# The last inverse unit of a fused SSM convolution: two writes and two of its four reads issued from ScalarE's queue

## The chip, the core and the metric

The kernel runs on one core of one Trainium2 chip, as a single launch in float32. The metric is the device time of that launch in microseconds. One execution is also recorded by the profiler, and the places below are given in microseconds from the start of that recording.

## The reference

Two S4 layers (A and B) convolve the same input `u` (2048 positions, 512 channels) with kernels built from 128 complex states each, and a gate mixes the two results:

```python
dt = jnp.exp(log_dt)[:, None]
P = jnp.exp((dt * (A_re + 1j * A_im))[:, :, None] * l[None, None, :])
K = jnp.einsum("dn,dnl,dn->dl", Cc, P, dt * Bc).real
Kf, Uf = rfft(K, 2 * L), rfft(u, 2 * L)          # zero-padded to twice the length
y = irfft(Uf * Kf, 2 * L)[..., :L] + u * Dskip
...
g = sigmoid((x * gate_w).sum(-1, keepdims=True))
return g * a + (1 - g) * b
```

## The kernel before

The 512 channels are worked in eight chunks (`c` from 0 to 7) of 64 channels, both layers together. For each chunk `tables` builds the time kernels (POOL, ScalarE and VectorE make sines and exponentials, TensorE multiplies them), `first` and `spectrum` transform them in two stages, `conv` multiplies with the spectrum of `u`, and `back` and `fin` transform back. All of that is interleaved over the chunks.

The end of the last chunk (`c` = 7) is what the change touches. `back(7, U)` for the units `U` = 0 to 3 does the first half of the inverse transform: 64 matmuls (`L721`) into a pair of PSUM banks, two copies (`L300` on ScalarE or `L302` on VectorE) into the tile `z`, two DMA writes of 256 KB each from `z` into the scratch `zb` in device memory, and then reads of `zb` back into SBUF in another layout, into the tile that is called `xa` here. Units 0 to 2 are read whole, 512 KB each. Unit 3, the last, is read in four quarters of 128 KB, one for each of the four final matmul groups. `fin(7, k)` is such a group: 32 matmuls (`L757`, `c<-xa,gsi`) that need the quarter `k` of unit 3 and the whole of units 0 to 2, then one copy, then one DMA of 128 KB to the output. The groups run as `k` = 3, 2, 1, 0. The outputs of chunk 6 (`fin(6, k)`, matmuls `c<-f,gsi`) are finished in the same stretch. Between them `stay_awake` runs twelve matmuls (`L770`) whose result nobody reads.

Nothing is scheduled by rule here. Every operation is recorded with a number by `Plan.__call__`, and the table of numbers `ORDER` gives the one order in which all are laid down; each engine takes its own in that order. An operation with two engines to choose from runs on the second if its number carries a `b`. In the tail, 1879 and 1880 are the two writes of unit 3; 1869 is the whole read of unit 2; 1884, 1883, 1882 and 1881 are the quarters 3, 2, 1 and 0 of unit 3; 1968, 1959 and 1965 are the output DMAs of chunk 6 for `k` = 3, 0 and 2, and 1962 the one for `k` = 1.

All DMAs are issued by SyncE (SP in the profile), but for those that `dma` is told may go to ScalarE (ACT):

```python
op("sp act" if also_act else "sp", "dma", size,
   lambda e: (sp if e == "sp" else act).dma_start(out=out(), in_=in_()), reads, writes, touch=touch)
```

A queue issues in order: an instruction that waits holds everything behind it on its engine. Eight semaphores (`DMAHW0` to `DMAHW7` in the instructions' waits) are dealt to the DMAs of both queues in rotation, and a DMA is issued only when the DMA that had its semaphore before it has landed. So a DMA can wait for one whose data it doesn't use.

Of the kernel before, what the change touches and what calls it, by code (L numbers as in the profile page):

```python
# [150 lines left out]
1811 1380 1394 1406 1382 1812 1407 1408 1820 1819 1837 1785 1798 1846 1802 1803 1800 1813 1801 1814 1947 1395b 1396 1873 1956  # L151
1849 1818 1786 1788 1409b 1410 1381b 1411 1821 1825 1413 1826b 1828 1412 1827 1829 1817 1816 1815 1787 1835 1836 1838 1847
1850 1839 1840 1862 1859 1841 1848 1851 1852 1842 1853 1854 1863 1860 1831 1832 1843 1844 1833 1830 1874 1871 1864 1957 1855
1856 1845 1865 1875 1872 1866 1876 1867 1868 1857 1877 1878b 1960 1966 1967b 1981 1963 1968b 1958b 1964b 1879 1880 1869 1884
1978 1883 1959 1975 1882 1965b 1972 1881 1961 1962 1969 1979 1980 1976 1973 1977 1970 1974 1971
"""


# [49 lines left out]
def ssm_mix(ctx: ExitStack, tc: tile.TileContext, a, out, dry=False):  # L208
# [58 lines left out]
    def t(*key):  # L267
        if key not in tiles:
            shape, dtype = shapes[key[0]]
            tiles[key] = pools[key[0]][slot[key]].tile(shape, dtype, name=key[0])  # L270
        return tiles[key]
# [21 lines left out]
    def dma(size, out, in_, reads, writes, also_act=False, touch=()):  # L293
        op("sp act" if also_act else "sp", "dma", size,
           lambda e: (sp if e == "sp" else act).dma_start(out=out(), in_=in_()), reads, writes, touch=touch)

    def copy(n, o, i, reads, writes, touch=()):
        def emit(e):
            if e == "act":
                act.activation(out=o(), in_=i(), func=AF.Copy)  # L300
            else:
                dve.tensor_copy(out=o(), in_=i())  # L302

        op("act dve", "copy", n, emit, reads, writes, touch=touch)
# [402 lines left out]
    def back(c, U):  # L707

        last = c == NCH - 1
        ys = [("y", c, 2 * U + i) for i in range(2)]  # L710
        ps = [(("s", "sq")[U % 2], "inv", U)] if last else [("c", "inv", c, U, x) for x in range(2)]
        bank_of = lambda x: t(*ps[0]).rearrange("p a b -> p (a b)")[:, 512 * x:512 * x + 512] if last else t(*ps[x])

        def inv(_):
            for q in range(4):
                for h in range(2):
                    for x in range(2):
                        for e in range(2):
                            f = 2 * q + e
                            v = t("vv", U // 2)[64 * x:64 * x + 64, 8 * (U % 2) + f]  # L720
                            pe.matmul(bank_of(x)[64 * e:64 * e + 64, CH * q:CH * q + CH], v[:, 0:64] if h else v[:, 32:96],  # L721
                                      t(*ys[f // 4])[64 * x:64 * x + 64, h, :, f % 4], start=h == 0, stop=h == 1,
                                      tile_position=(64 * x, 64 * e))

        op("pe", "inv", 128, inv, [*ys, ("vv", U // 2)], ps, table="square")
        z, zb, f = ("z", c, U), ("zb", c), home(c)
        for x in range(2):
            copy(512, lambda x=x: t(*z)[:, x].rearrange("p q k -> p (q k)"), lambda x=x: bank_of(x), [ps[0 if last else x]],
                 [z] * (x == 0) + [("zx", c, U, x)], [z] * x)
        new = U == 0  # L730
        for x in range(2):
            g = 8 * U + 4 * x
            dma(256, lambda g=g: t(*zb)[g:g + 4].rearrange("g p k -> p g k"), lambda x=x: t(*z)[:, x],
                [("zx", c, U, x)], [zb] * (new and x == 0) + [("zu", c, U, x)], touch=[z] + [zb] * (not (new and x == 0)))
        whole = last and U < 3
        for h in range(1 if whole else 4):
            a0, an = (0, 32) if whole else (8 * h, 8)
            dma(512 if whole else 128, lambda a0=a0, an=an: t(*f)[32 * U:32 * U + 32, a0:a0 + an],
                lambda a0=a0, an=an: t(*zb)[8 * U:8 * U + 8].rearrange("g (m a) k -> (g m) a k", m=4)[:, a0:a0 + an],
                [("zu", c, U, 0), ("zu", c, U, 1)],  # L740
                [f] * (new and h == 0) + [("fu", c, U, i) for i in (range(4) if whole else (h,))],
                touch=[zb] + [f] * (not (new and h == 0)))

    def home(c):
        return ("f", c) if c < NCH - 1 else ("xa", "fin")
# [49 lines left out]
    for T in range(NT):  # L795
        c, g = divmod(T, NG)
# [8 lines left out]
    for c in range(NCH):  # L805
        for j in range(NJ):
            conv(c, j)
            if j % 2:
                back(c, j // 2)
# [48 lines left out]
```

## Time and profile before

| | us |
|---|---|
| median of 3 runs | 434.33 (433.04 to 438.38) |
| the profiled execution's own time | 429.2 |
| its span, first to last instruction | 427.4 |
| busy in the span: PE / DVE / ACT / POOL | 384.0 / 385.1 / 361.3 / 358.7 |
| granted TensorE clock, mean | 0.994 |

The profiled execution was quicker than the three runs. Its span leaves out 1.8 us around the first and last instruction. Until about 396 us all four engines are nearly always busy. In the last 15.4 us (412.0 to 427.4) PE is busy 9.81 us, DVE 0.66 and ACT 1.92, and what is left is writes, reads and outputs.

In the rows below, `SPq` and `ACTq` are DMA issues from SyncE and ScalarE, with the time of issue and how long the issuing took. A row of DMA issues has a count, the KB of each, and the time from issue to landing.

### The profile page before, as it was taken

What the parts mean: (1) busy time and instruction counts of PE and PEld (TensorE: products, weight loads), DVE (VectorE), ACT (ScalarE), POOL (GpSimd) and SP (SyncE); (2) the same over time, 40 slices, a digit from 0 to 9 for tenths busy, and PEclk for the clock granted to TensorE, in tenths of its full rate; (3) what the DMA queues carried; (4) which work ended last, traced back from release to release, by engine and by line L of the source; (5) the groups of instructions that cost most, each with busy time, mean ns of one, the idle gap of its engine ahead of it and who ended that gap; (6) DMA issues with size and microseconds to landing.
All of it is one profiled execution on the core that took longest, in us unless ns stands there. A gap on an engine that the chain in (4) does not pass through costs nothing.

```text
span 427.4 us, 21919 instructions
## 1 busy us (share of the span) xinstructions
PE 384.0 (90%) x9636; PEld 342.3 (80%) x9636; DVE 385.1 (90%) x547; ACT 361.3 (85%) x522; POOL 358.7 (84%) x291
## 2 busy tenths in 40 slices
PE   5898887899998989998989999999889979999994
PEld 5787776788877878888979988888778969898964
DVE  5799999999999999998989999999999999996620
ACT  2889999899998999998889989999899898992211
POOL 1896989899999999997999999999999999970000
PEclk9999999899999999999999999999999999999999
DMA  7968845178882677687385555574777576667794
GB/s 240 287 214 269 263 149 180 28 221 224 257 247 79 197 215 203 201 240 230 109 221 177 176 170 156 166 220 145 225 209 217 143 220 199 172 205 216 219 274 137
DMA packets 79855, 84.63 MB, mean 198 GB/s; under 512 B 7600, under 2 KB 62768, under 8 KB 79664
## 3 DMA queue, kind: packets, MB, share of 16 engines
q1 hardware_dynamic: 79472, 82.96, 65.9%
q8 instruction: 76, 1.25, 1.3%
q10 hardware_dynamic: 288, 0.26, 0.2%
q14 instruction: 19, 0.16, 0.1%
HBM read 51.55 MB, written 31.65 MB: 195 GB/s over the span
## 4 chain that ended last, share of the span: by engine, by line
PE 32%; ACT 23%; DVE 15%; POOL 11%; issue 10%; DMA 7%; SPq 1%; ACTq 0%; DVEq 0%; POOLq 0%
PE c L625 8%; PE c L612 8%; PE c L721 6%; PE c L595 5%; POOL ang L277 4%; DVE mr L287 4%; ACT s L290 4%; POOL mr L277 4%; ACT sq L290 4%; ACT ang L290 3%; PE c L757 3%; DVE ei L277 3%; ACT z L300 2%; DMA zb<-z 2%; DVE y L701 2%
## 5 line engine op out<-in xcount | busy, mean ns | idle before, releaser
L287 DVE SCALAR_TENSOR_TENSOR mr<-sq,mr 128x1024 f32<-128x1024 f32 (+1 forms) x128 | 117.5, 946 | 3.1 <-ACT sq L290 3.0
L277 POOL TENSOR_TENSOR mr<-ml 128x1024 f32<-128x1024 f32 x52 | 101.6, 1955 | 2.5 <-PE c L595 2.0
L277 DVE TENSOR_TENSOR ei<-s,mr 128x1024 f32<-128x1024 f32 x64 | 77.6, 1213 | 2.6 <-POOL mr L277 1.0
L595 PE MATMUL c<-mr 128*32 128x64 f32 x2048 | 64.5, 223 | 8.0 <-DVE mr L287 3.0
L290 ACT ACTIVATE s<-ang 128x1024 f32<-128x1024 int32 x64 | 66.2, 1035 | 6.0 <-DVE ei L287 3.4
L277 POOL TENSOR_TENSOR ang<-sa 128x512 int32<-128x512 int32 x64 | 69.8, 1092 | 0.3
L277 POOL TENSOR_TENSOR ang<-par,cint 128x512 int32<-128x512 int32 x64 | 67.2, 1052 | 3.1 <-ACT sq L290 3.1
L701 DVE TENSOR_TENSOR y<-c,u 128x1024 f32<-128x1024 f32 x57 | 68.7, 1214 | 1.1 <-PE c L625 0.8
L290 ACT ACTIVATE ang<-ang 128x1024 f32<-128x1024 int32 x64 | 67.9, 1061 | 0.9
L290 ACT ACTIVATE sq<-ang 128x1024 f32<-128x1024 f32 x64 | 66.1, 1033 | 2.9 <-DVE mr L287 1.5
L277 POOL TENSOR_TENSOR mr<-mh 128x512 f32<-128x512 f32 x64 | 68.3, 1071 | 0.0
L595 PE MATMUL c<-ei 128*32 128x64 f32 x2048 | 63.6, 221 | 1.4 <-issue 1.4
L612 PE MATMUL c<-small,kt 128*64 128x128 f32 x1024 | 63.0, 275 | 1.6 <-ACT z L300 0.9
L595 PEld LDWEIGHTS c<-mr 128*32 128x32 f32 x2048 | 48.4, 110 | 19.0 <-issue 10.0
L721 PE MATMUL c<-y,vv 64*64 64x128 f32 x1792 | 57.9, 273 | 3.9 <-issue 2.6
L612 PEld LDWEIGHTS c<-small,kt 128*64 128x64 f32 x1024 | 55.5, 137 | 5.4 <-ACT z L300 1.3
L625 PE MATMUL c<-xa,w 128*128 128x128 f32 x384 | 53.0, 284 | 4.6 <-ACT z L300 2.3
L721 PEld LDWEIGHTS c<-y,vv 64*64 64x64 f32 x1792 | 50.1, 133 | 8.4 <-issue 3.7
L625 PE MATMUL c<-xb,w 128*128 128x128 f32 x384 | 51.9, 283 | 5.3 <-DVE c L420 1.6
L625 PEld LDWEIGHTS c<-xb,w 128*128 128x128 f32 x384 | 45.7, 191 | 10.7 <-issue 2.4
L625 PEld LDWEIGHTS c<-xa,w 128*128 128x128 f32 x384 | 45.9, 191 | 9.4 <-ACT z L300 2.9
L595 PEld LDWEIGHTS c<-ei 128*32 128x32 f32 x2048 | 50.4, 111 | 1.6 <-issue 1.5
(108 smaller groups left out, 594.5 us busy)
## 6 DMA issues: line engine op xcount, KB each, us to landing
zb<-z SPq DMA_DIRECT2D x64, 256.0 KB, 3.6
u<-us SPq DMA_DIRECT2D x57, 256.0 KB, 4.1
f<-zb SPq DMA_DIRECT2D x112, 128.0 KB, 3.9
us<-z SPq DMA_DIRECT2D x32, 256.0 KB, 3.1
uin<-in_uk_dram SPq DMA_DIRECT2D x16, 256.0 KB, 4.1
f<-in_ut_dram SPq DMA_DIRECT2D x8, 512.0 KB, 5.6
out_dram<-o SPq DMA_DIRECT2D x28, 128.0 KB, 3.2
par<-prd SPq DMA_DIRECT2D x7, 320.0 KB, 4.2
```

Source lines behind the costliest of these rows:

```text
L277: lambda e: (dve if e == "dve" else pool).tensor_tensor(out=out(), in0=in0(), in1=in1(), op=o),
L287: lambda _: dve.scalar_tensor_tensor(out=out(), in0=in0(), scalar=s, in1=in1(), op0=o0, op1=o1), reads, writes, port=port)
L290: op("act", "act", n, lambda _: act.activation(out=out(), in_=in_(), func=func, **{k: v() if callable(v) else v for k, v in kw.items()}), ...
L300: act.activation(out=o(), in_=i(), func=AF.Copy)
L595: pe.matmul(ps[32 * j:32 * j + 32, o], x[:, 4 * o + j, 64:96], x[:, 4 * o + j, 0:64], start=part == 0, stop=part == 1, tile_position=(0, 3 ...
L612: pe.matmul(t(*ps[g // 4])[64 * r:64 * r + 64, 128 * (g % 4):128 * (g % 4) + 128], t(*x)[:, g], t("small")[:, 128 * r:128 * r + 128], star ...
L625: pe.matmul(view()[:, :, k], t("w2", j // 2)[:, 4 * (j % 2) + k], t(*x1)[:, 4 * j + k], start=True, stop=True)
L701: op("dve", "tt1", 1024, lambda _: dve.tensor_tensor(out=t(*y).rearrange("p h s f d -> p h s (f d)"), in0=fv().rearrange("p s f d -> p s ( ...
L721: pe.matmul(bank_of(x)[64 * e:64 * e + 64, CH * q:CH * q + CH], v[:, 0:64] if h else v[:, 32:96], t(*ys[f // 4])[64 * x:64 * x + 64, h, :, ...
L757: pe.matmul(t(*ps)[64 * r:64 * r + 64, DC * i:DC * i + DC], t("gsi")[:, 4 * k + i, s, 64 * r:64 * r + 64], t(*f)[:, 8 * k + 2 * i + r, DC ...
```

## The change

The two writes of unit 3 may now be issued by ScalarE, and they are: they stand behind the one of the two `z` copies of that unit that ScalarE makes. Of the four quarter reads 1883 and 1881 (`k` = 2 and 0) go to ScalarE's queue too, 1884 and 1882 stay on SyncE's. The outputs of chunk 6 keep their engines but stand elsewhere: 1968 behind the writes on ScalarE, 1959 behind the quarter reads on SyncE, 1965 behind the quarter reads on ScalarE. The data, the sizes and the matmuls are the same.

```diff
-1856 1845 1865 1875 1872 1866 1876 1867 1868 1857 1877 1878b 1960 1966 1967b 1981 1963 1968b 1958b 1964b 1879 1880 1869 1884
-1978 1883 1959 1975 1882 1965b 1972 1881 1961 1962 1969 1979 1980 1976 1973 1977 1970 1974 1971
+1856 1845 1865 1875 1872 1866 1876 1867 1868 1857 1877 1878b 1960 1966 1967b 1981 1963 1958b 1879b 1880b 1968b 1964b 1869 1884
+1978 1883b 1975 1882 1972 1881b 1959 1965b 1961 1962 1969 1979 1980 1976 1973 1977 1970 1974 1971
...
             dma(256, lambda g=g: t(*zb)[g:g + 4].rearrange("g p k -> p g k"), lambda x=x: t(*z)[:, x],
-                [("zx", c, U, x)], [zb] * (new and x == 0) + [("zu", c, U, x)], touch=[z] + [zb] * (not (new and x == 0)))
+                [("zx", c, U, x)], [zb] * (new and x == 0) + [("zu", c, U, x)],
+                last and U > 2, touch=[z] + [zb] * (not (new and x == 0)))
...
-                [f] * (new and h == 0) + [("fu", c, U, i) for i in (range(4) if whole else (h,))],
+                [f] * (new and h == 0) + [("fu", c, U, i) for i in (range(4) if whole else (h,))], last and U == 3,
                 touch=[zb] + [f] * (not (new and h == 0)))
```

On SyncE's queue near the program's end there stood, before, from the writes of unit 2 (out of `z_7576`) over the whole read of unit 1 and the writes of unit 3 (out of `z_7619`) to the whole read of unit 2 and the four quarter reads:

```order
L295 DMA zb_7507<-z_7576 128x4x128 [waits DMAHW1_49,Activation_49]
L295 DMA zb_7507<-z_7576 128x4x128 [waits Activation_49]
L295 DMA xa_7574<-zb_7507 32x4096 [waits DMAHW7_49,DMAHW6_49]
L295 DMA zb_7507<-z_7619 128x4x128 [waits DMAHW5_49,Activation_49]
L295 DMA zb_7507<-z_7619 128x4x128 [waits DVE_49]
L295 DMA xa_7574<-zb_7507 32x4096 [waits DMAHW2_49,DMAHW1_49,DMAHW0_49]
L295 DMA xa_7574<-zb_7507 32x1024 [waits DMAHW7_49,DMAHW5_49]
L295 DMA xa_7574<-zb_7507 32x1024
L295 DMA out_0_dram<-o_7683 128x256 [waits DMAHW3_49,DVE_49]
L295 DMA xa_7574<-zb_7507 32x1024 [waits DMAHW4_49]
L295 DMA xa_7574<-zb_7507 32x1024
```

The whole read of unit 2, the second `32x4096` row, waited for the two writes of unit 2 (`DMAHW1` and `DMAHW2`) and for the DMA that had its own semaphore before it, `DMAHW0`, which is the whole read of unit 0. At the same place there stands now:

```order
L295 DMA zb_7507<-z_7576 128x4x128 [waits Activation_49]
L295 DMA zb_7507<-z_7576 128x4x128 [waits DMAHW4_49,Activation_49]
L295 DMA xa_7574<-zb_7507 32x4096 [waits DMAHW7_49,DMAHW6_49,DMAHW5_49]
L295 DMA xa_7574<-zb_7507 32x4096 [waits DMAHW4_49,DMAHW2_49,DMAHW1_49]
L295 DMA xa_7574<-zb_7507 32x1024 [waits DMAHW3_49]
L295 DMA xa_7574<-zb_7507 32x1024
L295 DMA out_0_dram<-o_7682 128x256 [waits DMAHW5_49,DVE_49]
```

The writes of unit 3 and two quarters are gone from this queue. The writes of unit 2 now carry `DMAHW2` and `DMAHW4`, and the whole read of unit 2 waits for these and for `DMAHW1`. On ScalarE's queue at the end, from the copy of unit 3 into `z_7619` on, the difference is:

```order
 L300 ACTIVATE z_7619<-sq_7583 128x512 [waits DMAHW6_49,DMAHW7_49,PE_49,Activation_49]
-L295 DMA out_0_dram<-o_7656 128x256 [waits DMAHW4_49,DVE_49]
-L295 DMA out_0_dram<-o_7685 128x256 [waits DVE_49]
-L300 ACTIVATE o_7747<-c_7622 128x256 [waits DMAHW5_49,DMAHW3_49,PE_49]
+L295 DMA zb_7507<-z_7619 128x4x128 [waits DMAHW1_49,Activation_49]
+L295 DMA zb_7507<-z_7619 128x4x128 [waits DVE_49]
+L295 DMA out_0_dram<-o_7656 128x256 [waits DVE_49]
+L295 DMA xa_7574<-zb_7507 32x1024 [waits DMAHW3_49,DMAHW1_49]
+L295 DMA xa_7574<-zb_7507 32x1024 [waits DMAHW0_49]
+L295 DMA out_0_dram<-o_7687 128x256 [waits DMAHW2_49,DVE_49]
+L300 ACTIVATE o_7747<-c_7622 128x256 [waits DMAHW5_49,PE_49]
```

Here `DMAHW1` and `DMAHW3` are the two writes of unit 3, since the quarter read behind them waits for both. The first write holds `DMAHW1`, the semaphore for which the whole read of unit 2 on the other queue waits too: in the rotation that read comes eight DMAs behind it, and the count it asks for is the one that this write brings.

## The prediction

> **What bounds the kernel now.** I read the stretches first, to see where in the span this change lies.
>
> ```profile
> core 0: us, PE busy (x) PEld busy (x) DVE busy (x) ACT busy (x) POOL busy (x), PEclk, DMA share, GB/s
> 0.00:380.00 380.00, 342.84 (x8704) 306.99 (x8707) 363.52 (x520) 347.91 (x498) 356.89 (x290) 1.00 0.67 197
> ...
> 412.00:427.40 15.40, 9.81 (x172) 6.65 (x170) 0.66 (x2) 1.92 (x5) 0.00 (x0) 0.96 0.60 175
> ```
>
> For 380 us the engines themselves are the limit, and nothing there is touched. What the change can move lies in the last 15.4 us, where VectorE and ScalarE have hardly any work. Then I read the chain of waits of that end.
>
> ```profile
> 407.51 1.95 PE sq L721 x64
> ...
> 409.53 0.60 ACT z L300
> 410.14 0.02 issue
> 410.16 0.70 DVE z L302
> 410.86 0.02 issue
> 410.88 5.03 DMA zb<-z
> ...
> 416.85 2.74 DMA out_dram<-o
> ...
> 419.65 3.96 PE c L757 x128
> ```
>
> Last inverse matmuls, two copies, second write of unit 3 (5.03 us), reads of it, last four matmul groups: from 409.5 to 419.65 the kernel waits for transfers. The step through the output at 416.85 I don't believe, since no matmul needs an output. What the matmuls at 419.65 need are the whole reads and quarter 3. So I asked for the issues one by one, from SyncE's queue and ScalarE's:
>
> ```profile
> 410.15 0.36 SPq L295 DMA_DIRECT2D zb<-z  x1
> 410.88 0.39 SPq L295 DMA_DIRECT2D zb<-z  x1
> 411.94 0.38 ACTq L295 DMA_DIRECT2D out_dram<-o  x1
> 412.97 0.32 SPq L295 DMA_DIRECT2D xa<-zb  x1
> 415.97 0.32 SPq L295 DMA_DIRECT2D xa<-zb  x1
> 416.34 0.41 SPq L295 DMA_DIRECT2D xa<-zb  x1
> 416.85 0.37 SPq L295 DMA_DIRECT2D out_dram<-o  x1
> 417.27 0.42 SPq L295 DMA_DIRECT2D xa<-zb  x1
> 417.74 0.41 SPq L295 DMA_DIRECT2D xa<-zb  x1
> 418.36 0.34 ACTq L295 DMA_DIRECT2D out_dram<-o  x1
> ```
>
> These are write 1 and write 2 of unit 3, an output, the whole read of unit 2, quarters 3 and 2, an output, quarters 1 and 0, an output. The DMA issues of a narrow window give the time to landing of the first five of them, in the same order:
>
> ```profile
> zb<-z SPq DMA_DIRECT2D x1, 256.0 KB, 5.1
> zb<-z SPq DMA_DIRECT2D x1, 256.0 KB, 5.0
> out_dram<-o ACTq DMA_DIRECT2D x1, 128.0 KB, 4.4
> xa<-zb SPq DMA_DIRECT2D x1, 512.0 KB, 5.8
> xa<-zb SPq DMA_DIRECT2D x1, 128.0 KB, 3.4
> ```
>
> So write 1 lands at 410.15 + 5.1 = 415.25, write 2 at 415.9, the output at 416.3, the whole read of unit 2 at 412.97 + 5.8 = 418.8, quarter 3 at 415.97 + 3.4 = 419.4, and the matmuls start 0.25 later. Each lands behind the one issued before it: quarter 3 comes 0.6 behind the whole read of unit 2. The end of the kernel hangs on that whole read nearly as much as on the writes.
>
> **The change part by part.**
>
> *The two writes on ScalarE.* The copy on ScalarE ends at 409.53 + 0.60 = 410.13 and write 1 is issued at 410.15; VectorE's ends at 410.86 and write 2 is issued at 410.88. There are 0.02 us to win at each, and issuing costs 0.38 on ScalarE against 0.36 and 0.39 here. Write 2 waits for VectorE's copy on either queue. I take 0.
>
> *Their landing.* If the two queues share one line of work, 415.25 and 415.9 stay. Whether ScalarE's queue gets past SyncE's is told by its output at 411.94: it took 4.4 us where the same size later takes
>
> ```profile
> out_dram<-o SPq DMA_DIRECT2D x1, 128.0 KB, 1.8
> out_dram<-o ACTq DMA_DIRECT2D x1, 128.0 KB, 2.9
> ```
>
> (issued at 421.28 and at 418.36). With 2.9 it would have landed at 414.8; it landed at 416.3, 0.4 behind write 2, which SyncE had issued 1.06 before it. So ScalarE's queue did not overtake, and I take 0.
>
> [...]
>
> *The new wait.* The whole read of unit 2 stays on SyncE. Before it was issued at 412.97, just when the second write of unit 2 had landed; now it asks for write 1's semaphore as well and can't be issued before 415.25: 2.28 us later. Behind it on SyncE stand quarters 3 and 1, which wait for write 2 until 415.9 anyway, and all later outputs. The cost is less than 2.28, because of its 5.8 us much was queueing behind the writes (2.9 us, until 415.9). The other two whole reads, issued at 405.25 and 408.17, and the write in front of the first, issued at 403.76, give the scale:
>
> ```profile
> xa<-zb SPq DMA_DIRECT2D x1, 512.0 KB, 5.3
> xa<-zb SPq DMA_DIRECT2D x1, 512.0 KB, 6.4
> zb<-z SPq DMA_DIRECT2D x1, 256.0 KB, 3.3
> ```
>
> The first took 5.3 with 1.8 us of queue in front (that write landed at 407.06). After the change there is 1.05 in front (the output until 416.3). If queueing counts one to one, the read takes 5.3 - 1.8 + 1.05 = 4.55 and lands at 419.8, against 418.8: +1.0. Lower bound: nothing in front counts, 3.5 us, 418.75, no loss. Upper bound: 5.8 as now, 421.05, +2.25. I take +1.0, from the read with the queue most like it.
>
> *The reads of unit 3.* Two queues issue the quarters two at a time, quarters 3 and 2 at about 415.95 and quarters 1 and 0 at about 416.35, where the last went at 417.74 before. Nothing waited for these in the old trace:
>
> ```profile
> 419.65 3.95 PE L757 MATMUL c<-xa,gsi 128*64 128x64 f32 x128 [1.79 <-DMA out_dram<-o]
> ```
>
> 128 matmuls took 3.95 us in one piece, so earlier quarters 2, 1 and 0 gain 0. Quarter 3 can't land before the whole read in front of it and keeps its 0.6 behind it. A cost could be that quarter 2 gets in front of quarter 3: at most one quarter's share of the line, 0.3 us (quarters 3 and 2, issued 0.37 apart, take the same 3.4 us). I take 0 and keep 0.3 for the range.
>
> *The outputs of chunk 6.* ScalarE's queue now stands still from about 412.3 until write 2 has landed. Behind it are an output and the copies of the end:
>
> ```profile
> 417.90 0.42 DVE L302 COPY o<-c 128x256 f32<-128x256 f32 x1 [5.67 <-PE c L757]
> 420.09 0.38 ACT L300 ACTIVATE o<-c 128x256 f32<-128x256 f32 x1 [9.96 <-DMA xa<-zb]
> ```
>
> That output has its data at 418.32 and the reads are issued by 416.75, so 1.6 us of cover remain; without it each us lost there would come on top. The copy at 420.09 needs the slot that output 1959 frees; this stood at 416.85 and will stand at about 416.75, behind quarter 1. Even if it lands as late as the reads do (+1.0), the copy goes at 421.1, before the first of the last groups is done at 419.65 + 1.0 + 1.0. 0. The last output is issued by SyncE at
>
> ```profile
> 424.10 0.78 SPq L295 DMA_DIRECT2D out_dram<-o  x1
> out_dram<-o SPq DMA_DIRECT2D x1, 128.0 KB, 2.2
> ```
>
> right behind its copy, and moves with the matmuls. It lands after 2.2 where 1.8 is the quickest; with the earlier outputs more spread up to 0.4 may come back. I take 0.
>
> **Sum.** Writes 0, whole read of unit 2 +1.0, quarters 0, outputs 0: +1.0 us. Matmuls at 420.65, span 428.4, the profiled execution 429.2 + 1.0 = 430.2. That execution lies 5.1 below the median of the runs shown (434.33). The end of the program has no reason to cost more in those, so the forecast is 434.33 + 1.0 = 435.3. That is 0.2%, far inside the 2% that a measurement of this kernel can tell from no change.
>
> **The rivals.**
>
> [...]
>
> *Late* (clearly slower). The reads of the end are all issued within 1.5 us, from 415.25 to 416.75, on two queues, where they were spread over 4.8 us. If the whole read keeps 5.8 although less stands in front of it and quarter 2 gets in front of quarter 3, matmuls start 2.25 + 0.3 = 2.55 later: 436.9. It is decided by the whole read taking more than 5.3. Against it: there is 1.85 us less in front of it.
>
> *Hidden.* Without the queue the whole read of unit 2 takes 3.5 and lands where it did: 434.3. This is the low end of the sum, and for it speaks that the writes are out of its way.
>
> **How the numbers follow.** Forecast (+0.4 to +1.8) 0.50, hidden 0.16, turns 0.20, late 0.14. The predicted time is that of the forecast, 435.3. The three runs differ by 5.3 us, more than any of the cases. Low end: turns 433.6, less the 0.4 of the last output and the 1.3 by which the quickest of the runs lies below the median, 432.0 (rounded up from 431.9). High end: the forecast plus half the runs' spread, 435.3 + 2.65 = 438.0, which takes in late. Within 2% means 425.6 to 443.0: no case comes near either end, and I keep 0.01 for faster and 0.02 for slower for what the rows don't show.
>
> **What would show it.** Right: write 1 issued at 410.15 by ScalarE and landing 5 us later; the whole read of unit 2 issued when write 1 lands, no longer at 412.97; quarter 3 at 415.9 landing last; the 128 matmuls at 420.65 in one piece; a gap on ScalarE between its output at 411.94 and the quarter reads. [...] Wrong, towards late: the whole read taking over 5.3 us, or the 128 matmuls broken by a wait for a quarter. Wrong altogether: matmuls starting before 418.9, or a difference that arises before 409 us, where the two programs are the same.

## The result and the profile after

The changed kernel takes 436.69 us (median of 22 executions, 432.77 to 442.49) where the kernel before took 433.23 beside it (22 executions, 430.45 to 439.39). The ratio is 1.0058, 95% interval 1.0033 to 1.0084: about 2.5 us slower, well inside 2%, but the interval leaves out 1. The ratios here leave out executions more than 1.5% above the quickest of their kernel, so that they are not the quotients of the two medians. The prediction had the direction and less than half of the size (+1.0 us).

The profiled execution of the changed kernel took 434.64 us, with a span of 432.8. Not all of the 5.4 us against the span before is the change. ScalarE's copy of the last unit, in front of which the two programs are the same, came at 409.53 before and comes 2.97 us later here:

```profile
412.50 0.60 ACT L300 ACTIVATE z<-sq 128x512 f32<-128x512 f32 x1 [1.90 <-issue]
413.12 0.41 ACTq L295 DMA_DIRECT2D zb<-z  x1
413.85 2.62 ACTq L295 DMA_DIRECT2D zb<-z  x1
416.51 0.78 ACTq L295 DMA_DIRECT2D out_dram<-o  x1
417.91 0.32 SPq L295 DMA_DIRECT2D xa<-zb  x1
418.62 0.30 SPq L295 DMA_DIRECT2D xa<-zb  x1
```

These are, from the timelines of ScalarE and of SyncE, the copy, write 1, write 2, output 1968, the whole read of unit 2 and quarter 3. I count all that follows from the copy. The DMA issues of narrow windows give the landing of write 1, write 2, the whole read, quarter 3, output 1959 and the last output:

```profile
zb<-z ACTq DMA_DIRECT2D x1, 256.0 KB, 4.8
zb<-z ACTq DMA_DIRECT2D x1, 256.0 KB, 4.8
xa<-zb SPq DMA_DIRECT2D x1, 512.0 KB, 5.2
xa<-zb SPq DMA_DIRECT2D x1, 128.0 KB, 5.1
out_dram<-o SPq DMA_DIRECT2D x1, 128.0 KB, 6.2
out_dram<-o SPq DMA_DIRECT2D x1, 128.0 KB, 1.7
```

Write 1 lands at 413.12 + 4.8 = 417.9, and at 417.91 the whole read of unit 2 is issued: 5.41 us behind the copy, where it was 412.97 - 409.53 = 3.44 before. The wait is there, and it costs 1.97 us at the issue. The whole read lands at 423.1, quarter 3 at 423.7. The matmuls follow (the timelines of PE; the second fence has the windows of the clock's grid, with the time in the window, the busy time of PE and the granted clock `PEclk`):

```profile
419.67 1.15 PE L758 MATMUL c<-f,gsi 128*64 128x64 f32 x32
423.96 5.50 PE L758 MATMUL c<-xa,gsi 128*64 128x64 f32 x128 [3.14 <-DMA xa<-zb]
```

```profile
core 0: us, PE busy (x), PEclk, DMA share, GB/s
418.14:421.56 3.42, 2.69 (x36) 1.00 0.83 195
421.56:424.97 3.41, 1.01 (x34) 1.00 0.91 204
424.97:428.38 3.41, 3.41 (x71) 0.50 0.34 110
428.38:431.80 3.42, 1.08 (x35) 1.00 0.28 92
```

(Lines of the changed kernel are one higher from the edit on: `L757` is `L758`.) The same 128 matmuls that took 3.95 us now take 5.50, in one piece, with no wait inside. At 424.97, one microsecond after they begin, the granted clock goes to 0.50 for 3.41 us. Before, it stood at 1.00 through all of them:

```profile
core 0: us, PE busy (x), PEclk, DMA share, GB/s
415.86:419.27 3.41, 2.00 (x35) 1.00 0.64 172
419.27:422.69 3.42, 3.04 (x104) 1.00 0.36 119
422.69:426.10 3.41, 0.92 (x32) 1.00 0.48 156
```

From the copy to the end of the span it was 17.88 us and is 20.27. The 2.39 us are made up so:

| us behind the copy on ScalarE | before | after | difference |
|---|---|---|---|
| whole read of unit 2 issued | 3.44 | 5.41 | +1.97 |
| it lands | 9.28 | 10.58 | +1.30 |
| last 128 matmuls start | 10.12 | 11.46 | +1.34 |
| time of these matmuls | 3.95 | 5.50 | +1.55 |
| from their end to the end of the span | 3.81 | 3.31 | -0.50 |

So the matmuls start 1.34 later, they take 1.55 longer at the lower clock, and 0.50 comes back at the last output, which lands in 1.7 us instead of 2.2. The sum agrees with the 2.5 us of the timed runs, but it is one execution each: a second profile of the changed kernel, after2 below, has 21.64 us from the copy to the end. What the experiments had to tell is whether the wait is the cause, whether the clock falls because of it, and whether the two queues themselves cost anything.

### The profile page after: what moved, and what is told of

It is laid out like the page before. It is cut to its first block, busy times and chain, and to the rows that moved or that the text cites. A ratio compares the mean times of both kernels' runs of the same rounds, so it can differ in the third digit from the quotient of the medians.

```text
span 432.8 us, 21920 instructions
## 1 busy us (share of the span) xinstructions
PE 387.5 (90%) x9636; PEld 345.1 (80%) x9636; DVE 385.2 (89%) x547; ACT 361.2 (83%) x522; POOL 358.8 (83%) x291
## 4 chain that ended last, share of the span: by engine, by line
PE 37%; ACT 24%; DVE 15%; issue 10%; POOL 7%; DMA 6%; SPq 1%; DVEq 0%; ACTq 0%; POOLq 0%
PE c L612 11%; PE c L625 7%; PE c L595 6%; PE c L721 5%; PE c L758 5%; DVE mr L287 4%; ACT s L290 4%; ACT sq L290 4%; POOL mr L277 3%; DVE ei L277 3%; POOL ang L277 3%; ACT z L300 3%; ACT ang L290 3%; DVE y L701 2%; ACT mh L531 2%
```

## The experiments

In all of them the times are set against the kernel before, run beside them on the same chip. A number such as 1982 in an edit of `ORDER` is a new operation. The profiled executions differ by up to 9 us ahead of the tail (ScalarE's copy comes at 409.53 to 418.65), and for that reason places in the tail are told as distances from that copy. Of a line of `ORDER` only the numbers around the edit are shown.

**Each half of the change alone.** The first kernel, e_writes, has the writes on ScalarE and all reads as before:

```diff
-1958b 1879b 1880b 1968b 1964b 1869 1884 1978 1883b 1975 1882 1972 1881b 1959 1965b
+1958b 1879b 1880b 1968b 1964b 1869 1884 1978 1883 1959 1975 1882 1965b 1972 1881
```

> The changed kernel with all four quarters and output 1959 on SP in the order of before: of the change only the two writes on ScalarE's queue are left, ahead of output 1968. The whole read of unit 2 gets another semaphore here and does not wait for write 1. Theory: within 0.5 us of the kernel before; write 1 and write 2 land 5 to 6.5 us behind the copy as in both kernels, the 128 matmuls take 4.0 us. Rival 'queue': +1.5 to +2.5 us, with the second write's issue of 2.6 us on ScalarE in front of output 1968. Rival 'quarters': as before, since nothing of the reads is changed; it can't be told from the theory here.

433.65 us, ratio 0.9998 (0.9965 to 1.0032). The second, e_reads, has the reads of the changed kernel and the writes as before:

```diff
-1963 1958b 1879b 1880b 1968b 1964b 1869
+1963 1968b 1958b 1964b 1879 1880 1869
```

> The changed kernel with the two writes on SP behind output 1968 as before: of the change only quarters 2 and 0 on ScalarE's queue with output 1959 behind them are left. The whole read of unit 2 does not wait for a write of unit 3. Theory: within 0.5 us of the kernel before. Rival 'quarters' (four quarters over two queues land later or in another order than the matmuls use them, and break the 128 matmuls): +1 to +2.5 us, with the matmuls' block at 5 us or more. Rival 'queue': within 0.5 us.

434.46 us, ratio 1.002 (0.9986 to 1.0053). Neither half, by its median, costs what the whole does, though the interval of e_reads still allows 0.5%. In both, the dealing of the semaphores comes out so that the whole read of unit 2 doesn't wait for a write of unit 3; in e_writes it is issued 3.46 us behind the copy, 3.44 before. The last matmuls in the timelines of PE, of e_writes and then of e_reads:

```profile
428.45 3.95 PE L758 MATMUL c<-xa,gsi 128*64 128x64 f32 x128 [1.47 <-DMA xa<-zb]
```

```profile
428.58 3.95 PE L758 MATMUL c<-xa,gsi 128*64 128x64 f32 x128 [2.01 <-DMA xa<-zb]
```

With the copy at 418.65 and 418.24 they start 9.80 and 10.34 us behind the copy, 10.12 before, and take the 3.95 us of before. That speaks against the rival that put the cost on the quarters over two queues, and against a cost of ScalarE's queue as such; the times of e_reads alone don't settle the first, e_split below does more.

**The wait in the kernel before.** The kernel b_wait is the kernel before with a transfer of four bytes on SyncE that reads what write 1 writes:

```diff
-1964b 1879 1880 1869
+1964b 1879 1880 1982 1869
...
+dma(1, lambda: t("dummy")[0:1], lambda: t("zb", NCH - 1)[24][0:1, 0:1], [("zu", NCH - 1, 3, 0)], [("dummy",)])
```

> The kernel before, and a transfer of one number on SP in front of the whole read of unit 2, which reads from what write 1 writes and so makes SP stand until write 1 has landed: the wait alone, with both writes, all quarters and all outputs as before. Theory (the wait for write 1 is what costs, directly and through the half clock behind it): the read is issued about 2.5 us later than in the kernel before, TensorE's idle time ahead of the last matmuls is 3 us or more, and the time is +1.5 to +3 us, with 1 to 1.7 us of it lost to the half clock (the runs' mean clock: 2.8 us lost in the 35 executions of the kernel before, 4.5 in the 22 of the changed kernel). Rival 'late write' (the second write's slow issue on ScalarE, 1.8 to 2.6 us in all four traces that have it, is what costs, since quarter 3 waits for that write; the wait is hidden behind it): within 0.5 us.

436.39 us, ratio 1.0083 (1.0047 to 1.012). With writes and reads on the queues where they were, this costs as much as the whole change, or more. SyncE's timeline shows write 1, the four bytes, the whole read and quarter 0, PE's, in the second fence, the last matmuls:

```profile
411.75 0.36 SPq L295 DMA_DIRECT2D zb<-z  x1
416.50 0.29 SPq L295 DMA_DIRECT2D dummy<-zb  x1
416.88 0.33 SPq L295 DMA_DIRECT2D xa<-zb  x1
423.92 0.30 SPq L295 DMA_DIRECT2D xa<-zb  x1
```

```profile
422.85 5.50 PE L757 MATMUL c<-xa,gsi 128*64 128x64 f32 x128 [3.40 <-DMA xa<-zb]
```

The copy is at 411.12 here: the read is issued 5.76 us behind it, the matmuls start 11.73 behind it and take 5.50. Both terms of the changed kernel's tail are there again, +1.61 and +1.55. It is not the wait quite alone: the added transfer takes a place in the dealing of the semaphores, and quarter 0 is issued only when an output on ScalarE's queue has landed, 12.80 us behind the copy instead of 8.21. In this profile no matmul waited for it, but a part of the +0.8% can be its own.

**The wait taken out of the changed kernel.** In e_free a transfer of one number on ScalarE's queue shifts the rotation of the semaphores by one:

```diff
-1958b 1879b 1880b 1968b 1964b 1869
+1958b 1879b 1880b 1968b 1982b 1964b 1869
...
+dma(1, lambda: t("dummy")[0:1], lambda: a["gate_w"][0:1, 0:1], (), [("dummy",)], True)
```

> The changed kernel, and a transfer of one number on ScalarE's queue behind output 1968, into a tile that nobody reads. It takes a place in the rotation of the eight semaphores, so that the whole read of unit 2 no longer shares one with write 1 and waits for its own unit's writes alone; writes, quarters and outputs stay as the change puts them. Theory (of the 2.4 us that the tail of the changed kernel is longer, 1.3 are the wait for write 1, 1.55 the half clock that follows the longer idle time of TensorE, and -0.5 the last output): the read is issued within 0.3 us of its own writes' landing, the last unit's 128 matmuls take 4.0 us at clock 1.0 after an idle time of about 1.8 us, and the time is within 0.5 us of the kernel before. Rival 'queue' (the writes on ScalarE, with an issue of 2.6 us for the second, cost it): still +2 us or more. Rival 'quarters' (the reads over two queues cost it): still +2 us or more.

434.92 us, ratio 1.0051 (1.0016 to 1.0086): a miss. The wait is gone in the profile, and the tail is no shorter. ScalarE's and SyncE's timelines have write 2, the whole read, the added transfer and quarter 3, and the DMA issues the time to landing of write 2:

```profile
418.65 1.82 ACTq L295 DMA_DIRECT2D zb<-z  x1
419.66 0.32 SPq L295 DMA_DIRECT2D xa<-zb  x1
421.06 2.86 ACTq L295 DMA_DIRECT2D dummy<-in_gate_w_dram  x1
426.89 0.30 SPq L295 DMA_DIRECT2D xa<-zb  x1
```

```profile
zb<-z ACTq DMA_DIRECT2D x1, 256.0 KB, 8.2
```

The copy was at 417.30, so the whole read goes 2.36 us behind it, against 3.44 before and 5.41 in the changed kernel. But ScalarE takes 1.82 us to issue write 2, until 420.47, and by then the read is ahead of it. Write 2 takes 8.2 us, and quarter 3, which needs it, is issued only at 426.89. TensorE stands idle for 4.11 us and the matmuls take 6.59. So there is a second weakness in the changed kernel that the wait covers: a slow issue of write 2. In e_writes the same slow issue (two writes in 2.74 us) cost nothing, since there the read came at 422.11, behind it. This rests on one profile, and the added transfer held ScalarE for 2.86 us itself; what share of the +0.5% is its own stays open.

**Write 2 on SyncE, write 1 on ScalarE.** In e_split all else is as in the changed kernel; the whole read doesn't wait for unit 3:

```diff
-1958b 1879b 1880b 1968b 1964b 1869
+1958b 1879b 1880 1968b 1964b 1869
...
-                last and U > 2, touch=
+                last and U > 2 and x == 0, touch=
```

> The changed kernel with write 2 on SP and only write 1 on ScalarE's queue; quarters 2 and 0 and output 1959 stay as changed. The whole read of unit 2 does not wait for a write of unit 3 here. Both the theory and the rival 'late write' expect write 2 to be issued in about 0.4 us, the read right behind it as in the kernel before, TensorE's idle time near 1.8 us and the time within 0.7 us of the kernel before. Rival 'quarters' (reads over two queues): +1.5 us or more.

433.64 us, ratio 0.9977 (0.9938 to 1.0017). The same kernel once more, beside split_warm below:

> The kernel e_split once more, beside split_warm. Theory: 0.996 to 1.000 of the kernel before, between the kernel before and split_warm.

432.44 us, ratio 1.0004 (0.9964 to 1.0044). Write 2 is issued in 0.36 us, the last matmuls start 10.33 and 9.96 us behind the copy (PE's timelines, e_split and then split2):

```profile
425.65 5.50 PE L758 MATMUL c<-xa,gsi 128*64 128x64 f32 x128 [2.00 <-DMA xa<-zb]
```

```profile
421.36 3.95 PE L758 MATMUL c<-xa,gsi 128*64 128x64 f32 x128 [1.64 <-DMA xa<-zb]
```

Without the wait and without the slow issue the loss is gone in the timed runs, with the quarters still over two queues. But in the first of the two profiles the last matmuls took 5.50 us all the same: the half clock can come without the wait too.

**The clock alone.** Matmuls whose result nobody reads, in front of the last 128, so that TensorE is not idle while it waits. They go into the bank of the stay-awake matmuls:

```diff
-1981 1963 1958b
+1981 1963 1982 1958b
...
+op("pe", "warm", 24, lambda _: [pe.matmul(t("c", "awake"), t("w2", 0)[:, 0], ...) for _ in range(n)], ...)
```

> The changed kernel with four matmuls more (0.59 us each, into the bank of the stay-awake matmuls, which nobody reads) behind the product matmuls of chunk 6, in TensorE's idle time ahead of the last unit's matmuls. The wait for write 1 stays. Theory: TensorE's idle time ahead of the last matmuls falls from 3.1 to about 0.8 us, the clock stays 1.0, the 128 matmuls take 4.0 instead of 5.5 us, and the time is +0.8 to +1.2 us against the kernel before instead of +2.5. If the block was long because matmuls waited for quarters, and not for the clock: the block stays at 5.5 us and the time at +2.5. If the clock falls by chance in every kernel alike, the time also stays at +2.5.

With four of them (e_warm) 435.63 us, ratio 1.0052 (1.0015 to 1.0088). PE's timeline has the added matmuls and the last 128:

```profile
419.54 3.70 PE L816 MATMUL c<-w,w 128*128 128x512 f32 x8
423.30 3.95 PE L758 MATMUL c<-xa,gsi 128*64 128x64 f32 x128
```

The last ones take 3.95 us, as the theory says, but the time hardly falls: each added matmul counts as two records of 0.6 us, they last until 423.24, and the last 128 start 12.02 us behind the copy (at 411.28) instead of 11.46. The expectation forgot that cover which is too long becomes a delay: quarter 3, issued at 418.17, had landed after 4.4 us, at 422.6. With two of them (e_warm2), and the changed kernel again beside it (after2):

> The changed kernel with two matmuls more instead of four (four profile records of 0.6 us) in TensorE's idle time ahead of the last matmuls, so that they are over before the data land. Theory: idle time about 0.8 us less than 1.7 in one piece, clock 1.0 there, 3.95 us for the 128 matmuls, the clock's mean loss over the runs as in the kernel before (2.8 us instead of 4.5), and the time 1 to 2 us under that of the changed kernel of the same call, +0.8 to +1.5 us against the kernel before. If the half clock is no cause: the same as the changed kernel of the same call.

> The changed kernel once more, beside the others of this call. Theory: +1.5 to +3.5 us; the whole read again issued right behind write 1's landing, with TensorE's idle time ahead of the last matmuls at 3 us or more; whether the clock is halved at the last matmuls depends on where the 3.41 us grid of the clock changes falls in this execution.

The changed kernel gave 435.22 us, ratio 1.0059 (1.0028 to 1.009), with two matmuls more it gave 433.55, ratio 1.0015 (0.9982 to 1.0048). The timelines of PE, of after2 and then of e_warm2:

```profile
424.41 6.51 PE L758 MATMUL c<-xa,gsi 128*64 128x64 f32 x128 [3.53 <-DMA xa<-zb]
```

```profile
423.20 1.98 PE L816 MATMUL c<-w,w 128*128 128x512 f32 x4
426.57 3.95 PE L758 MATMUL c<-xa,gsi 128*64 128x64 f32 x128 [1.39 <-DMA xa<-zb]
```

The wait is in both; the matmuls start 11.86 and 11.62 us behind the copy. In after2 the half clock lasted two windows, 6.83 us, and the matmuls took 6.51. With the idle time cut to 1.39 us the half clock is gone, and the ratio falls from 1.0059 to 1.0015, though the two intervals overlap. The same two matmuls in b_wait (b_wait_warm):

> The kernel with the wait alone (b_wait), and two matmuls more (four profile records of 0.6 us) in TensorE's idle time ahead of the last matmuls. Theory: the wait stays and with it some 1.0 to 1.5 us, the half clock goes: idle time in one piece near 1.0 us instead of 3.4, 3.95 us for the 128 matmuls, mean loss to the clock below 3 us instead of 5.4, and the time +0.8 to +1.8 us against the kernel before, where b_wait had 1.0083 of it. If the half clock is no cause: 1.008 as b_wait.

434.67 us, ratio 1.003 (0.9998 to 1.0062) where b_wait had 1.0083 (1.0047 to 1.012). As expected, but for the idle time, which was 1.82 us, and for a break of the last matmuls by a late quarter:

```profile
429.20 3.02 PE L757 MATMUL c<-xa,gsi 128*64 128x64 f32 x96 [1.82 <-DMA xa<-zb]
432.58 1.15 PE L757 MATMUL c<-xa,gsi 128*64 128x64 f32 x32 [0.36 <-DMA xa<-zb]
```

The executions that the ratios rest on point the same way. Time lost to the clock, (1 - mean granted clock) x span, is 2.30 us on average in 76 executions of the kernel before, 4.12 in 30 of the changed kernel, 5.43 in 8 of b_wait, and 1.59 in 12 of e_warm2 and 2.08 in 10 of b_wait_warm. It counts half clock in idle time too, so the 1.8 us between the first two are an upper measure of what it cost.

The tails of the profiles, though, don't show the gain. From the copy to the end of the span it is 20.07 us in e_warm, 20.36 in e_warm2 and 20.72 in b_wait_warm, against 20.27 and 21.64 in the changed kernel and 20.69 in b_wait. In b_wait_warm the late quarter takes a part. And some of what the matmuls save goes again behind them: from their end to the end of the span it is 3.26 to 3.46 us in the five profiles where they ran at half clock (after, after2, e_free, e_split, b_wait), and 3.81 to 5.34 in the nine where they did not. The outputs follow closer on each other then: the first four of the last five are issued within 1.4 us in e_warm2, 1.8 in the kernel before and 2.8 in the changed kernel. In e_warm2 ScalarE's last copy waits for one of them:

```profile
432.13 0.38 ACT L300 ACTIVATE o<-c 128x256 f32<-128x256 f32 x1 [2.12 <-DMA out_dram<-o]
```

So the 0.50 that came back in the changed kernel belongs with the 1.55, which is no net price. The half clock is in all three profiles with the wait and no added matmuls, and in none of the three with both; how much of the 2.5 us the clock makes stays open. e_warm2 and b_wait_warm speak for 1.9 and 2.3 us by their ratios, with intervals that overlap those of the kernels without the added matmuls; e_warm gained next to nothing.

**A better version.** One matmul more in the kernel before (b_warm), and one in e_split (split_warm):

> The kernel before with one matmul more (two records of 0.6 us) in TensorE's idle time of 1.8 us ahead of the last matmuls. If the idle time of the kernel before is now and then long enough for the half clock: 0.3 to 1 us faster than the kernel before. If it never is: the same within 0.3 us.

433.33 us, ratio 0.9999 (0.9966 to 1.0032): no gain shows there.

> The kernel e_split (write 1 on ScalarE, write 2 on SP, quarters over two queues) with one matmul more in TensorE's idle time of 2.0 us ahead of the last matmuls, which was long enough for the half clock in e_split's profile (5.50 us for the 128 matmuls). Theory: 3.95 us for them, and 0.5 to 2 us faster than the kernel before. If the half clock is no cause: as e_split (0.998).

432.53 us, ratio 0.9972 (0.9948 to 0.9996). TensorE is idle for 0.53 us ahead of the last matmuls, and they take 3.95. It is the only kernel here whose interval lies below the kernel before, by little. What of it is the matmul and what the queues can't be told from split2, whose interval covers it.

## Why the prediction was right or wrong

*Writes on ScalarE, issue 0.* Wrong for write 2, without a price of its own in the changed kernel. It took 2.62 us to issue, against 0.39 on SyncE. I had read the issue of an output from ScalarE, 0.38 us, as the price of any. ScalarE's queue therefore got to output 1968 4.0 us behind the copy instead of 2.4, for which nobody waited. e_free, a single profile, shows where it can cost.

*Their landing 0.* Right. From the copy, write 1 landed after 5.40 us (5.69 before) and write 2 after 6.11 (6.38). In after2 it was 5.69 and 6.37, as before. The 4.4 us of the output at 411.94, from which I took that ScalarE's queue doesn't overtake, agrees with that. The low end of the range starts from 433.6 for *turns*, and no run shows that term: it wanted the writes to land well sooner than in the kernel before, and counted from the copy write 1 came 0.3 us sooner in one profile of the changed kernel and no sooner in the other.

*The new wait +1.0.* Right in mechanism, short in size: the last matmuls moved by 1.34 us, and by 1.74 in after2. The issue moved by 1.97, not 2.28, since write 1 came a little sooner (by 2.26 in after2); the read took 5.2 us in both, not the 4.55 that I had worked out by counting the queue in front one to one. The rows of the kernel before were against that count already: three reads took 5.3, 5.8 and 6.4 us with 1.8, 2.9 and 4.7 us of queue in front (in front of the third, issued at 408.17, a write issued at 407.65 that took 5.2 us, until 412.85), and less the queue that is 3.5, 2.9 and 1.7, not one number. *Hidden*, which had the read at 3.5 us, falls with these 5.2.

*Quarters 0, outputs of chunk 6 0.* Right for the end. Quarter 3 kept its 0.6 us behind the whole read, and e_reads shows no clear loss (1.002, 0.9986 to 1.0053). The cover that I named for ScalarE's copies is gone, though: output 1959 took 6.2 us, and the copy that waits for its slot went 13.3 us behind the copy of the last unit, not 11.6 as I had worked out. The copies behind it caught up before the last group.

*Last output 0, bound -0.4.* -0.50 in this execution, with the outputs more spread because the matmuls in front of them ran slower.

*The sum.* Here is the step that failed. I had the matmuls start 1.0 later and the span end 1.0 later, so that the block of 128 matmuls kept its 3.95 us. It took 5.50, and 6.51 in after2. The longer wait in front of TensorE was not only a delay: it left 1.01 us busy in the window from 421.56 to 424.97, and the granted clock in the next was 0.50. The row that I quoted had the idle time in it, 1.79 us, and I read it as slack only.

*Late* gave 436.9, close to what was measured, by another way: it wanted a read of more than 5.3 us or a block broken by a quarter, and neither is in the profile. That a rival's number fits is no support for its mechanism. Nor is it the merit of the sum that 436.69 lies within 432.0 to 438.0: the high end was the forecast plus half the spread of three runs, and that room took in a term which the sum didn't have.

## What to carry to other kernels

Where an engine waits for transfers at the end of a kernel, price a longer wait twice: as the delay (1.34 us here), and as what the idle time does to the clock of the matmuls behind it (1.55 here). Follow the sum to the end of the program, since slower matmuls can spare the transfers behind them some time again (0.50 here). When DMAs move between queues, look at the instructions' waits and not at the data alone: a semaphore that is dealt in rotation can tie a read to a write it has nothing to do with (here the read was issued 1.97 us later). And what looks like one fault may cover a second, so the cure of the one has to be run.

## What the runs showed of the hardware

In the profiles of the kernel before and of the changed kernel the granted clock of TensorE changes only on a grid of 3.41 us. Its place is another in each execution: an edge lies 6.33 us behind the copy in the kernel before, 5.64 in the changed kernel and, by the windows below, 7.10 in e_split and 6.54 in e_reads. In the first two, from 60 us on, the windows at full clock that were followed by half clock are the least busy ones. Two kernels with the same idle time in one piece show what the place does, e_split (2.00 us) and e_reads (2.01 us), by the windows of the grid:

```profile
422.42:425.83 3.41, 1.41 (x39) 1.00 0.90 206
425.83:429.24 3.41, 3.41 (x70) 0.50 0.24 78
```

```profile
424.78:428.19 3.41, 1.79 (x34) 1.00 0.89 194
428.19:431.61 3.42, 3.03 (x103) 1.00 0.22 70
```

In e_split the idle time lies whole in one window, 1.41 of 3.41 us are busy, and the clock is halved behind it: 5.50 us for the 128 matmuls. In e_reads the grid cuts the idle time, 1.79 us are busy, and it stays at 1.00: 3.95. The profiles of the kernel before and of the changed kernel have 106 windows each at full clock from 60 us to the last matmul. In the kernel before, two of them were followed by half clock, busy for 27% and 36% of the window, and the least busy of the others was busy for 59% (415.86 to 419.27). In the changed kernel it was three, busy for 29 to 32%, and the least busy of the others had 48% (216.76 to 220.17). With the 41% of e_split on one side and these 48% on the other, an idle time of 1.8 to 2.0 us in one window, an estimate from these shares, was enough in this kernel, and whether it falls into one window differs from execution to execution with the place of the grid.

The other surprise is the issue of a second write of 256 KB right behind a first on ScalarE's queue: 2.62 us in both profiles of the changed kernel, 1.82 in e_free, against 0.36 to 0.39 for write 2 on SyncE in the kernel before and in e_split (1.14 in b_wait). It is not ScalarE's alone: the second write of unit 1 took SyncE 1.31 us to issue in the kernel before (at 403.76) and 1.10 in the changed kernel (at 406.73). What holds an engine there no run tells; output 1968 behind the writes is issued only after it.
